# Transposes on TensorE from the third chunk on, filler matmuls in the first chunk, and one pool of four PSUM banks for the expert matmuls

## The chip, the cores and the metric

The kernel runs on one core of one Trainium2 chip. A core has five engines that this kernel uses: TensorE (PE) for matmuls, VectorE (DVE), ScalarE (ACT), GpSimd (POOL), and SyncE (SP), whose queue issues transfers. The metric is the device time of one execution in microseconds. Less is better. Three runs of the kernel before took 315.59, 315.67 and 315.96 us; the median is 315.67.

## The reference

Two stages follow each other. The first is a gated linear attention over 4 batches, 8 heads, 768 positions and a head size of 48. For each batch and head it keeps a 48 x 48 state:

```
f = sigmoid(f_logit)
for t in range(768):
    state = f[t][:, None] * state + outer(k[t], v[t])
    y[t]  = q[t] @ state
```

The 8 heads' outputs are put side by side, so that x has 4 x 768 = 3072 rows of 384. The second stage is a mixture of 4 experts, each with 1024 hidden units, in which every row goes through every expert:

```
p = domain_probs / (domain_probs.sum(-1) + 1e-9)
for e in range(4):
    out += p[:, e:e+1] * (relu(x @ w1[e]) @ w2[e])
```

Inputs and output are 32-bit floats in DRAM. The kernel casts operands of its matmuls to bf16 and accumulates in 32-bit.

## The kernel before

The 768 positions are cut into 6 chunks of 128. Within a chunk the attention is computed without a loop over positions: the logarithms of the gates are summed up by a matmul with a triangular matrix, queries are multiplied by the exponential of the sum and keys by its inverse, and two matmuls then give the chunk's output, with the state carried from chunk to chunk. Heads are handled in pairs, each padded to 64 columns, so a pair takes 112 partitions (MP).

One batch of one chunk goes through these steps (names of the plan, then the function):

- gate1, gate2 (ScalarE): log(1 + exp(-f)).
- cs (`pe_cs`, TensorE): cumulative sums, one matmul of 384 columns and, but for the last chunk, four of one column.
- exps (ScalarE): exponentials of both signs.
- q, k (`product`, L257, on GpSimd, or VectorE in chunks 0 and 1) and v (`cast_v`, L261): operands in bf16. The products of one batch share one padded tile `qk`; seven of these exist.
- The transpose of Q and K into the tile `QK`. In chunks 0 and 1 it is eight TensorE transposes (`pe_tp`, L265: tpq and tpk) into one PSUM bank and a copy by VectorE (ev_tp, L214). From chunk 2 on it is one DMA transpose from SP's queue (`dma_tp`, L269).
- at (`pe_at`, L280) and its masking by VectorE (ev_at, L284), y (`pe_y`, L291 and L295) and its cast to bf16 (ev_y).
- The transpose of the output into `xT`, the experts' operand. In chunks 0 and 1 it is three TensorE transposes (`pe_xt`, L320) and a copy (ev_xt, L212); from chunk 2 on one DMA transpose (`dma_xt`, L273).
- kv, ev_kv and state (`pe_kv`, L301, `ev_kv`, L308, `state`): the state for the next chunk.

The experts of one chunk work on all 512 rows (4 batches of 128). A unit h (`mm_h`, L324) is three matmuls of 512 columns into one PSUM bank, emptied by relu (`relu`, L332 on ScalarE, L330 on VectorE); in chunk 1 the first two experts are done in halves of 256 columns. A unit o (`mm_o`, L336) is four matmuls of 384 columns; two units with the same bank make one output tile, which `ev_o` (L343, L345, L347) scales and adds up. For one chunk that makes 32 h units (96 matmuls of 512 columns) and 32 o units (128 matmuls of 384 columns), which alternate over most of the span.

PSUM has eight banks, which the kernel hands out as rooms: two for h (`ps_h`), two for o (`ps_o`), four for the attention (`ps_t`).

The order is not written by hand. `Plan` is a small list scheduler that runs while the program is built. Each step has a cost in us for each engine that may do it, steps that it depends on, rooms that it takes and frees, a lag until its result can be used, and a priority. Going forward in planned time, `Plan.run` gives every idle engine the first step by priority whose inputs are there (0.2 us later for another engine, `LATENCY`) and whose rooms are free. The steps are then emitted in the order of planned start (L518 and after). The order on each engine's queue is thus the plan's; at run time an instruction waits for its inputs and everything behind it on that queue waits too.

The numbers of the plan that matter here: a load of one batch costs 1.05 us of DMA with a lag of 2.0, a gate step 0.54, cs 0.36, exps 1.1, the k product 0.56 on VectorE, tpq and tpk 0.22 each, at 0.35, y 0.28 in chunk 0 and 0.4 later, xt 0.17, kv 0.22, h 0.645, o 0.645, one expert weight 4.8 of DMA with a lag of 2.0.

`attention(c, ...)` adds a chunk's steps with priorities that spread them between the expert units of the chunk before; `zip_units` numbers those units. Chunk 0's attention has nothing to run beside. Its 16 loads of one batch each come first on SP's queue, the expert weights follow from GpSimd's queue after the last k load, and the loads of chunk 1 behind the sixth weight.

Of the kernel before, what the change touches and what calls it, by code (L numbers as in the profile page):

```python
# [14 lines left out]
class Op:  # L15


    def __init__(self, name, costs, emit, prio, deps=(), takes=(), frees=(), lag=0.0):
        self.name, self.costs, self.emit, self.prio = name, costs, emit, prio
        self.deps = [d for d in deps if d is not None]  # L20
        self.takes, self.frees, self.lag = list(takes), list(frees), lag
        self.end = self.start = self.engine = None


# [73 lines left out]
def kernel(  # L98
# [11 lines left out]
    nc = tc.nc  # L110
# [20 lines left out]
    ps = ctx.enter_context(tc.tile_pool(name="ps", bufs=1, space=PS))  # L131
    rooms = {"ps_h": 2, "ps_o": 2, "ps_t": 4, "f": 4, "q": 4, "k": 4, "v": 4, "ex": 2, "gp": 4, "e": 2, "qk": 7,
             "vb": 7, "egs": 8, "QK": 2, "AT": 2, "yb": 2, "xT": 2, "h": 2, "o": 8}
# [12 lines left out]
    pads = {}  # L146
    for nm, nb in (("gp", 2), ("qk", 2)):
        for i in range(rooms[nm]):
            t = pads[nm, i] = const.tile([T, nb, H, P2], BF16, name=f"{nm}{i}")
            nc.vector.memset(t[:, :, :, D:P2], 0.0)  # L150
# [22 lines left out]
    for nm, a in (("f", f_logit), ("q", q), ("k", k), ("v", v)):  # L173
# [5 lines left out]
        "ex": ([T, 2 * H, D], FP32), "e": ([T, 2, HD], FP32), "egs": ([MP, NP], FP32), "vb": ([T, H, D], BF16),  # L179
        "QK": ([128, 2, NP, T], BF16), "AT": ([T, 2, NP, T], BF16), "yb": ([T, HD], BF16),  # L180
        "xT": ([128, KD, NT], BF16), "h": ([128, KF, NT], BF16), "o": ([128, Din], FP32),
        "cs": ([T, 512], FP32), "tp": ([MP, 2, NP, T], BF16), "A": ([T, NP, T], FP32), "y": ([T, 512], FP32),
        "KV": ([T, 512], FP32), "xp": ([T, KD, T], BF16), "ps_h": ([128, NT], FP32), "ps_o": ([128, 512], FP32),
    }

    def tl(kind, *key):

        if (kind, key) not in tiles:
            room = kind if kind in rooms else "ps_t"
            slot = P.slot[(room, kind) + key if room == "ps_t" else (room,) + key]  # L190
            if room in ("gp", "qk"):
                tiles[kind, key] = pads[room, slot]
            else:
                shape, dt = shapes[kind]
                pool = ps if room.startswith("ps_") else wk
                tiles[kind, key] = pool.tile(shape, dt, name=f"{room}{slot}")
        return tiles[kind, key]
# [58 lines left out]
    def product(c, b, j, eng):  # L256
        engines[eng].tensor_tensor(out=tl("qk", c, b)[:, j, :, 0:D], in0=tl("qk"[j], c, b // 2)[:, hh(b), :],  # L257
                                   in1=tl("e", c, b)[:, j].rearrange("t (h d) -> t h d", d=D), op=ALU.mult)
# [4 lines left out]
    def pe_tp(c, b, j):  # L263
        for i in range(NP):
            nc.tensor.transpose(out=tl("tp", c, b)[:, j, i, :], in_=flat(tl("qk", c, b)[:, j], i)[:, 0:MP],  # L265
                                identity=ident)

    def dma_tp(c, b):
        nc.sync.dma_start_transpose(out=tl("QK", c, b).rearrange("m j i t -> m (j i) t"),  # L269
                                    in_=tl("qk", c, b).rearrange("t j h d -> t (j h d)"))  # L270

    def dma_xt(c, b):
        nc.sync.dma_start_transpose(out=tl("xT", c)[:, :, b * T:(b + 1) * T], in_=tl("yb", c, b))  # L273

# [12 lines left out]
    def pe_y(c, b):  # L287
        y, AT, vb, QK = tl("y", c, b), tl("AT", c, b), tl("vb", c, b), tl("QK", c, b)
        for i in range(NP):
            if c > 0:  # L290
                nc.tensor.matmul(out=y[:, i * 2 * D:(i + 1) * 2 * D], lhsT=QK[0:MP, 0, i, :],  # L291
                                 rhs=Sb[c % 2][:, b, i, :], start=True, stop=False, skip_group_check=True)
            for r in range(2):
                h = 2 * i + r
                nc.tensor.matmul(out=y[:, h * D:(h + 1) * D], lhsT=AT[:, r, i, :], rhs=vb[:, h, :],  # L295
                                 start=(c == 0), stop=True, skip_group_check=True)

    def pe_kv(c, b):
        kp, vb = tl("qk", c, b)[:, 1], tl("vb", c, b)
        for i in range(NP):  # L300
# [21 lines left out]
    def mm_h(c, e, fc, n0, n1):  # L322
        for kk in range(KD):
            nc.tensor.matmul(out=tl("ps_h", c, e, fc, n0)[:, n0:n1], lhsT=w1_sb[:, e, kk, fc * 128:(fc + 1) * 128],  # L324
                             rhs=tl("xT", c)[:, kk, n0:n1], start=(kk == 0), stop=(kk == KD - 1))

    def relu(c, e, fc, n0, n1, eng):
        dst, src = tl("h", c, e)[:, fc, n0:n1], tl("ps_h", c, e, fc, n0)[:, n0:n1]
        if eng == "DVE":
# [4 lines left out]
    def mm_o(c, e, nt, half):  # L334
        for fc in range(half * 4, half * 4 + 4):
            nc.tensor.matmul(out=tl("ps_o", c, e, nt)[:, 0:Din], lhsT=tl("h", c, e)[:, fc, nt * T:(nt + 1) * T],  # L336
                             rhs=w2_sb[:, e, fc, :], start=(fc == 0), stop=(fc == KF - 1))

    def ev_o(c, e, nt, eng):
        op, o = tl("ps_o", c, e, nt)[:, 0:Din], tl("o", c, nt)  # L340
        pe = pn[:, nt * C + c, e:e + 1]
# [39 lines left out]
    def attention(c, slot, gran):  # L381
# [10 lines left out]
        for b in range(B):  # L392
# [10 lines left out]
            qm = P.add(f"q {c}.{b}", pe, one(product, 0), s(4) - 0.2,  # L403
                       deps=[ex, ld[c, "q", b]], takes=[("qk", c, b)], frees=[("q", c, half), ("e", c, b)])
            km = P.add(f"k {c}.{b}", pe, one(product, 1), s(4) - 0.1,
                       deps=[ex, ld[c, "k", b]], takes=[("qk", c, b)], frees=[("k", c, half), ("e", c, b)])
            vb = P.add(f"v {c}.{b}", {"POOL": 0.5, "DVE": 0.36} if c < 2 else {"POOL": 0.5}, one(cast_v), s(4),
                       deps=[ld[c, "v", b]], takes=[("vb", c, b)], frees=[("v", c, half)])
            if c < 2:
                tq = P.add(f"tpq {c}.{b}", {"PE": 0.22}, on(pe_tp, 0), s(4), deps=[qm],  # L410
                           takes=[pt_("tp")], frees=[("qk", c, b)], lag=0.2)
                tk = P.add(f"tpk {c}.{b}", {"PE": 0.22}, on(pe_tp, 1), s(4) + 0.01, deps=[km],
                           takes=[pt_("tp")], frees=[("qk", c, b)], lag=0.2)
                et = P.add(f"ev_tp {c}.{b}", {"DVE": 0.69}, lambda e, b=b: copy(e, tl("QK", c, b)[0:MP], tl("tp", c, b)), s(4) + 0.1,
                           deps=[tq, tk], takes=[("QK", c, b)], frees=[pt_("tp")])
            else:
                et = P.add(f"tp {c}.{b}", {"DMA": 1.8}, on(dma_tp), s(4), deps=[qm, km], takes=[("QK", c, b)],
                           frees=[("qk", c, b)], lag=2.2)
            at = P.add(f"at {c}.{b}", {"PE": 0.35}, on(pe_at), s(7), deps=[et],
# [7 lines left out]
                       deps=[y], takes=[("yb", c, b)], frees=[pt_("y")])  # L427
            if c < 2:
                xt = P.add(f"xt {c}.{b}", {"PE": 0.17}, on(pe_xt), s(13), deps=[ey],
                           takes=[pt_("xp")], frees=[("yb", c, b)], lag=0.2)  # L430
                xdone[c, b] = P.add(f"ev_xt {c}.{b}", {"ACT": 0.48, "DVE": 0.4},
                                    lambda e, b=b: copy(e, tl("xT", c)[:, :, b * T:(b + 1) * T], tl("xp", c, b)),
                                    s(13) + 0.1, deps=[xt], takes=[("xT", c)], frees=[pt_("xp")])
            else:
                xdone[c, b] = P.add(f"xt {c}.{b}", {"DMA": 0.9}, on(dma_xt), s(13), deps=[ey], takes=[("xT", c)],
                                    frees=[("yb", c, b)], lag=2.2)
            if more:
                kv = P.add(f"kv {c}.{b}", {"PE": 0.22}, on(pe_kv), s(15), deps=[km, vb, y],
                           takes=[pt_("KV")], frees=[("vb", c, b), ("qk", c, b)], lag=0.2)
                ek = P.add(f"ev_kv {c}.{b}", {"DVE": 0.74}, on(ev_kv), s(15) + 0.1,  # L440
# [8 lines left out]
    def add_h(c, e, fc, n0, n1, xs):  # L449
        p, n = unit[0], n1 - n0  # L450
        key = ("ps_h", c, e, fc, n0)
        m = P.add(f"h {c}.{e}.{fc}.{n0}", {"PE": 0.645 * n / NT}, lambda _: mm_h(c, e, fc, n0, n1), p,
# [6 lines left out]
    def add_o(c, e, nt, half):  # L459
        p = unit[0] + 0.5  # L460
        key = ("ps_o", c, e, nt)
        d = [hdone[k] for k in hdone if k[:2] == (c, e) and half * 4 <= k[2] < half * 4 + 4 and k[3] <= nt * T]
# [47 lines left out]
    zip_units([], ol(C - 1, E - 1, ALL))  # L510

    done = P.run()
    if PRINT:
        PRINT(done)
    for o in done:
        o.emit(o.engine)

# [32 lines left out]
```

## Time and profile before

| what | value |
|---|---|
| median of three runs | 315.67 us |
| profiled execution | 315.96 us, its span 314.1 us |
| TensorE busy | 295.3 us, 94% of the span |
| ScalarE, VectorE, GpSimd busy | 163.0, 132.5, 92.6 us |
| first attention matmul | 4.89 us |
| first expert matmul | 25.38 us |
| DMA transposes | 16 into QK, 16 into xT |

PE is TensorE's matmuls, PEld its weight loads, which run beside matmuls. A matmul's duration in the profile includes the time in which its last results drain, in which the next one already runs; so the rate is read from starts, not durations. In a row of the timeline, the columns are the start, the duration from the first to the last instruction of a merged row, the engine, the line, the operation, output<-inputs, and the count; in square brackets stands the idle time before it and what ended it. In a table by stage each engine has its busy time and, in brackets, its number of instructions. The chain that ended last is a list of pieces: start, length, what.

### The profile page before, as it was taken

What the parts mean: (1) busy time and instruction counts of PE and PEld (TensorE: products, weight loads), DVE (VectorE), ACT (ScalarE), POOL (GpSimd) and SP (SyncE); (2) the same over time, 40 slices, a digit from 0 to 9 for tenths busy, and PEclk for the clock granted to TensorE, in tenths of its full rate; (3) what the DMA queues carried; (4) which work ended last, traced back from release to release, by engine and by line L of the source; (5) the groups of instructions that cost most, each with busy time, mean ns of one, the idle gap of its engine ahead of it and who ended that gap; (6) DMA issues with size and microseconds to landing.
All of it is one profiled execution on the core that took longest, in us unless ns stands there. A gap on an engine that the chain in (4) does not pass through costs nothing.

```text
span 314.1 us, 5415 instructions
## 1 busy us (share of the span) xinstructions
PE 295.3 (94%) x2098; PEld 171.1 (54%) x2128; DVE 132.5 (42%) x249; ACT 163.0 (52%) x310; POOL 92.6 (29%) x160
## 2 busy tenths in 40 slices
PE   1978999998999999999999999999999999999995
PEld 1753455556876555655555555555555555555552
DVE  6791002379954466443553222554332442201223
ACT  5634664554767563667544456443466444465430
POOL 4695000026996333860322200223322200000000
PEclk9999999999999999999999999999999999999999
DMA  8999999999999087999692113200322200200002
GB/s 156 211 150 192 196 208 201 208 202 214 189 223 236 6 172 140 230 197 189 108 196 48 50 50 48 46 15 13 95 75 46 50 13 15 75 25 2 0 0 100
DMA packets 135081, 36.05 MB, mean 115 GB/s; under 512 B 126352, under 2 KB 133520, under 8 KB 135056
## 3 DMA queue, kind: packets, MB, share of 16 engines
q1 hardware_dynamic: 129296, 29.42, 49.2%
q0 software_dynamic: 5760, 6.29, 12.0%
q8 instruction: 16, 0.26, 0.4%
q14 instruction: 9, 0.07, 0.1%
HBM read 31.51 MB, written 4.72 MB: 115 GB/s over the span
## 4 chain that ended last, share of the span: by engine, by line
PE 88%; DVE 7%; issue 2%; ACT 1%; DMA 1%; DVEq 0%; ACTq 0%
PE ps_h L324 40%; PE ps_o L336 39%; PE ps_t L280 2%; DVE qk L257 2%; DVE AT L284 2%; PE ps_t L295 1%; PE ps_t L244 1%; PE ps_t L291 1%; PE ps_t L301 1%; PE ps_t L247 1%; DMA f<-in_f_logit_dram 1%; PE ps_t L265 1%; DVE QK L214 1%; DVE o L343 1%; DVE vb L261 1%
## 5 line engine op out<-in xcount | busy, mean ns | idle before, releaser
L332 ACT ACTIVATE h<-ps_h 128x512 bf16<-128x512 f32 (+1 forms) x176 | 101.7, 579 | 111.2 <-PE ps_h L324 104.1
L324 PE MATMUL ps_h<-xT,w_sb 128*128 128x512 bf16 (+1 forms) x594 | 154.0, 367 | 2.9 <-ACT xT L212 0.6
L336 PE MATMUL ps_o<-w_sb,h 128*128 128x384 bf16 x768 | 153.0, 326 | 0.2
L336 PEld LDWEIGHTS <-h 128*128 128x128 bf16 x768 | 72.0, 98 | 56.8
L343 DVE SCALAR_TENSOR_TENSOR o<-ps_o,pn,o 128x384 f32<-128x384 f32 x72 | 44.4, 617 | 109.2 <-PE ps_o L336 101.9
L324 PEld LDWEIGHTS <-w_sb 128*128 128x128 bf16 x624 | 60.5, 99 | 50.9 <-issue 6.5
L284 DVE TENSOR_TENSOR AT<-ps_t,mask 128x512 bf16<-128x512 f32 x48 | 31.2, 684 | 14.8 <-PE ps_t L280 14.7
L261 POOL CAST vb<-v 128x384 bf16<-128x384 f32 x20 | 10.7, 537 | 72.9 <-DMA v<-in_v_dram 36.5
L257 POOL TENSOR_TENSOR qk<-q,e 128x384 bf16<-128x384 f32 x21 | 21.2, 1014 | 30.2 <-ACT e L251 29.9
L315 POOL TENSOR_TENSOR Sf<-Sf,egs 48x192 f32<-48x192 f32 x40 | 20.3, 508 | 24.6 <-DVE Sf L308 22.7
L330 DVE TENSOR_SCALAR h<-ps_h 128x256 bf16<-128x256 f32 (+1 forms) x32 | 17.4, 549 | 23.6 <-PE ps_h L324 23.2
L257 POOL TENSOR_TENSOR qk<-k,e 128x384 bf16<-128x384 f32 x19 | 19.3, 1015 | 21.8 <-ACT egs L254 11.3
L308 DVE TENSOR_TENSOR Sf<-Sf,ps_t 48x192 f32<-48x192 f32 x40 | 13.9, 349 | 10.7 <-PE ps_t L301 10.0
L251 ACT ACTIVATE e<-ps_t 128x384 f32<-128x384 f32 x24 | 11.8, 491 | 10.5 <-PE ps_t L247 4.6
L345 ACT ACTIVATE o<-ps_o,pn 128x384 f32<-128x384 f32 x22 | 12.8, 580 | 5.2 <-PE ps_o L336 4.5
L214 DVE CAST yb<-ps_t 128x384 bf16<-128x384 f32 x17 | 9.5, 556 | 13.8 <-PE ps_t L295 12.4
L316 POOL CAST sb<-Sf 48x192 bf16<-48x192 f32 x40 | 13.5, 339 | 2.6
L295 PE MATMUL ps_t<-vb,AT 128*128 128x48 bf16 x192 | 12.5, 190 | 1.5 <-DVE AT L284 1.4
L244 PE MATMUL ps_t<-gp,Ub 128*128 128x384 bf16 x24 | 8.5, 355 | 5.4 <-ACT gp L240 4.9
L295 PEld LDWEIGHTS <-AT 128*128 128x128 bf16 x192 | 10.5, 101 | 4.3 <-DVE AT L284 2.1
L252 ACT ACTIVATE e<-ps_t 128x384 f32<-128x384 f32 x24 | 11.9, 494 | 0.0
L236 ACT ACTIVATE ex<-f 128x768 f32<-128x768 f32 (+1 forms) x14 | 10.5, 753 | 1.9 <-DMA f<-in_f_logit_dram 1.7
(44 smaller groups left out, 138.7 us busy)
## 6 DMA issues: line engine op xcount, KB each, us to landing
w_sb<-in_moe_w_dram POOLq DMA_DIRECT2D x8, 768.0 KB, 20.9
out_dram<-o SPq DMA_DIRECT2D x24, 192.0 KB, 1.9
k<-in_k_dram SPq DMA_DIRECT2D x10, 384.0 KB, 5.3
f<-in_f_logit_dram SPq DMA_DIRECT2D x10, 384.0 KB, 5.6
q<-in_q_dram SPq DMA_DIRECT2D x10, 384.0 KB, 5.2
v<-in_v_dram SPq DMA_DIRECT2D x10, 384.0 KB, 5.8
f<-in_f_logit_dram SPq DMA_DIRECT2D x4, 192.0 KB, 3.9
k<-in_k_dram SPq DMA_DIRECT2D x4, 192.0 KB, 3.9
```

Source lines behind the costliest of these rows:

```text
L257: engines[eng].tensor_tensor(out=tl("qk", c, b)[:, j, :, 0:D], in0=tl("qk"[j], c, b // 2)[:, hh(b), :], in1=tl("e", c, b)[:, j].rearrange( ...
L261: engines[eng].tensor_copy(out=tl("vb", c, b), in_=tl("v", c, b // 2)[:, hh(b), :])
L284: nc.vector.tensor_tensor(out=tl("AT", c, b)[:, r].rearrange("s i t -> s (i t)"), in0=tl("A", c, b, r).rearrange("s i t -> s (i t)"), in1= ...
L295: nc.tensor.matmul(out=y[:, h * D:(h + 1) * D], lhsT=AT[:, r, i, :], rhs=vb[:, h, :], start=(c == 0), stop=True, skip_group_check=True)
L308: nc.vector.tensor_tensor(out=Sf[rows, b], in0=Sf[rows, b], in1=KV[rows, :, r, :], op=ALU.add)
L315: nc.gpsimd.tensor_tensor(out=Sf[rows, b], in0=Sf[rows, b], in1=eg, op=ALU.mult)
L316: nc.gpsimd.tensor_copy(out=nb[rows, b, :, r * D:(r + 1) * D], in_=Sf[rows, b])
L324: nc.tensor.matmul(out=tl("ps_h", c, e, fc, n0)[:, n0:n1], lhsT=w1_sb[:, e, kk, fc * 128:(fc + 1) * 128], rhs=tl("xT", c)[:, kk, n0:n1], s ...
L330: nc.vector.tensor_relu(out=dst, in_=src)
L332: nc.scalar.activation(out=dst, in_=src, func=AF.Relu)
L336: nc.tensor.matmul(out=tl("ps_o", c, e, nt)[:, 0:Din], lhsT=tl("h", c, e)[:, fc, nt * T:(nt + 1) * T], rhs=w2_sb[:, e, fc, :], start=(fc = ...
L343: nc.vector.scalar_tensor_tensor(out=o, in0=op, scalar=pe, in1=o, op0=ALU.mult, op1=ALU.add)
```

## The change

- Rooms: `ps_h` and `ps_o` become one room `ps_m` of four banks. An h unit takes one of these, an o unit too.
- The shared tile `qk` (7 of them) becomes two: `qp` (6) for queries and `kp` (7) for keys, each freed by its own last reader.
- `dma_tp` and `dma_xt` are gone. All chunks take the way that chunks 0 and 1 had: tpq, tpk, ev_tp, xt and ev_xt. `QK` has 112 partitions instead of 128.
- After planning, the new code walks through TensorE's steps in planned order up to the first h unit and puts filler matmuls before each of them: as many as the planned gap since the step before has multiples of 0.2 us, counted from 1.0 us. A filler is a 128 x 128 by 128 x 256 matmul of a constant tile `busy`, set to one by VectorE after the other constants, into the fourth of the `ps_m` banks. Nothing reads its result.

```diff
-    rooms = {"ps_h": 2, "ps_o": 2, "ps_t": 4, ..., "e": 2, "qk": 7,
+    rooms = {"ps_m": 4, "ps_t": 4, ..., "e": 2, "qp": 6, "kp": 7,
...
-    for nm, nb in (("gp", 2), ("qk", 2)):
+    for nm, nb in (("gp", 2), ("qp", 1), ("kp", 1)):
...
-    def dma_tp(c, b):
-        nc.sync.dma_start_transpose(out=tl("QK", c, b).rearrange("m j i t -> m (j i) t"),
-                                    in_=tl("qk", c, b).rearrange("t j h d -> t (j h d)"))
-
-    def dma_xt(c, b):
-        nc.sync.dma_start_transpose(out=tl("xT", c)[:, :, b * T:(b + 1) * T], in_=tl("yb", c, b))
...
-            if c < 2:
-                tq = P.add(f"tpq {c}.{b}", {"PE": 0.22}, on(pe_tp, 0), s(4), deps=[qm], ...)
-                tk = P.add(f"tpk {c}.{b}", {"PE": 0.22}, on(pe_tp, 1), s(4) + 0.01, deps=[km], ...)
-                et = P.add(f"ev_tp {c}.{b}", {"DVE": 0.69}, ...)
-            else:
-                et = P.add(f"tp {c}.{b}", {"DMA": 1.8}, on(dma_tp), s(4), deps=[qm, km], takes=[("QK", c, b)],
-                           frees=[("qk", c, b)], lag=2.2)
+            tq = P.add(f"tpq {c}.{b}", {"PE": 0.22}, on(pe_tp, 0), s(4), deps=[qm],
+                       takes=[pt_("tp")], frees=[("qp", c, b)], lag=0.2)
+            tk = P.add(f"tpk {c}.{b}", {"PE": 0.22}, on(pe_tp, 1), s(4) + 0.01, deps=[km],
+                       takes=[pt_("tp")], frees=[("kp", c, b)], lag=0.2)
+            et = P.add(f"ev_tp {c}.{b}", {"DVE": 0.69}, lambda e, b=b: copy(e, tl("QK", c, b), tl("tp", c, b)), s(4) + 0.1,
+                       deps=[tq, tk], takes=[("QK", c, b)], frees=[pt_("tp")])
...
-                xdone[c, b] = P.add(f"xt {c}.{b}", {"DMA": 0.9}, on(dma_xt), s(13), deps=[ey], takes=[("xT", c)],
-                                    frees=[("yb", c, b)], lag=2.2)
+            xt = P.add(f"xt {c}.{b}", {"PE": 0.17}, on(pe_xt), s(13), deps=[ey],
+                       takes=[pt_("xp")], frees=[("yb", c, b)], lag=0.2)
+            xdone[c, b] = P.add(f"ev_xt {c}.{b}", {"ACT": 0.48, "DVE": 0.4}, ...)
...
-        key = ("ps_h", c, e, fc, n0)
+        key = ("ps_m", "hp", c, e, fc, n0)
...
-        key = ("ps_o", c, e, nt)
+        key = ("ps_m", "op", c, e, nt)
...
     done = P.run()
+    first = next(o for o in done if o.name.startswith("h 0.")).start
+    busy = wk.tile([128, 256], BF16, name="busy")
+    nc.vector.memset(busy, 1.0)
+    spare = ps.tile([128, 512], FP32, name="ps_m3")
+    t = 1.0
+    for o in done:
+        if o.engine == "PE" and o.start <= first:
+            o.pad, t = int((o.start - t) / 0.2), o.end
     if PRINT:
         PRINT(done)
     for o in done:
+        for _ in range(o.pad):
+            nc.tensor.matmul(out=spare[:, 0:256], lhsT=busy[:, 0:128], rhs=busy, start=True, stop=True)
         o.emit(o.engine)
```

## The prediction

> **What bounds the kernel now.** I read the page's share of busy time and its 40 slices first, then busy time by stage, the order of instructions on TensorE, and the chain of waits in the first 26 us. Every time is us from the start of the one profiled execution: span 314.1, time 315.96, so 1.86 lies around the span; the median 315.67 is 0.29 (0.1%) lower.
>
> The page, with TensorE's and VectorE's slices of 7.85 us:
>
> ```profile
> PE 295.3 (94%) x2098; PEld 171.1 (54%) x2128; DVE 132.5 (42%) x249; ACT 163.0 (52%) x310; POOL 92.6 (29%) x160
> PE   1978999998999999999999999999999999999995
> DVE  6791002379954466443553222554332442201223
> PEclk9999999999999999999999999999999999999999
> ```
>
> TensorE is the resource; VectorE is full only in slices 2 and 3 and again in slices 8 to 10. Busy time by stage (engine by engine, then granted clock, DMA share, GB/s):
>
> ```profile
> 24.30:36.00 11.70, 10.79 (x37) 4.34 (x39) 0.62 (x3) 6.45 (x11) 4.07 (x10) 1.00 1.19 194
> 36.00:62.00 26.00, 25.84 (x140) 13.83 (x142) 3.72 (x7) 14.37 (x24) 0.50 (x1) 1.00 1.20 205
> 62.00:80.00 18.00, 16.06 (x178) 11.18 (x177) 15.83 (x28) 9.62 (x23) 8.80 (x13) 1.00 1.22 203
> 80.00:104.00 24.00, 23.33 (x217) 17.66 (x217) 13.79 (x32) 16.43 (x42) 17.98 (x27) 1.00 0.98 204
> 104.00:262.00 158.00, 156.90 (x1134) 87.00 (x1154) 69.69 (x123) 81.58 (x148) 44.40 (x78) 1.00 0.46 89
> ```
>
> The first number after each comma is TensorE. From 104 to 262, where nearly all of chunks 2 to 5's attention lies, it idles 1.10 us of 158. Work added to TensorE there lengthens the kernel by its own size; work taken from the DMA there is worth nothing. Before 24.3 TensorE waits for the first chunk's attention, a chain over all engines.
>
> **The transposes: about +9.6.** For each batch of chunks 2 to 5 (16 batches) the change removes two DMA transposes and adds on TensorE eight transposes of Q and K and three of x, with two evictions. Chunk 1 already does this, on a warm TensorE (start, duration, what):
>
> ```profile
> 74.16 0.61 PE L265 MATMUL ps_t<-ident,qk 128*112 128x128 bf16 x8
> 74.61 0.81 PE L336 MATMUL ps_o<-w_sb,h 128*128 128x384 bf16 x4
> ...
> 85.27 0.33 PE L320 MATMUL ps_t<-ident,yb 128*128 128x128 bf16 x3
> 85.44 0.49 PE L324 MATMUL ps_h<-xT,w_sb 128*128 128x256 bf16 x3
> ```
>
> A matmul's duration holds a drain that the next one overlaps, so I price by start to start: eight cost 74.61 - 74.16 = 0.45, three cost 0.17, a batch 0.62, sixteen 9.9. The same stretch's idle time could take up 1.1 at the very most; I let it take 0.3. Lower end 8.8, upper 9.9, I take 9.6.
>
> [...] The row gives 0.45/8 = 56 ns. [...]
>
> The evictions: the QK copy (0.68 on VectorE) and the xT copy (0.48 on ScalarE), 16 each, are 10.9 and 7.7 over 158 us in which the two are busy 69.7 and 81.6. They are hidden by the expert matmuls queued meanwhile. If one delayed an expert eviction so that both banks of its kind were full, TensorE would wait a fraction of a copy: 0 to 0.2 a batch, 0 to 3 in all. I take 0, since chunk 2's stage has idle engines and four shared banks tolerate more lateness. The DMA transposes leave SP's queue (issue 1.2 each, landing in 3.2 and 2.4), which frees loads and stores behind them; TensorE's waits in 104 to 262 name no transfer, so 0.
>
> **The head: fillers and a cold TensorE.** The clock row says full speed, but weight loads and spacing say otherwise:
>
> ```profile
> 30.02 0.15 PEld L324 LDWEIGHTS <-w_sb 128*128 128x128 bf16 x1 [0.28 <-issue]
> 30.45 0.15 PEld L324 LDWEIGHTS <-w_sb 128*128 128x128 bf16 x1 [0.28 <-issue]
> 30.88 1.01 PEld L324 LDWEIGHTS <-w_sb 128*128 128x128 bf16 x5 [0.28 <-issue]
> ```
>
> Until 30.88 a 512-column matmul takes 0.43 and its weight load 0.15; later 0.215 and 0.10. From the first expert matmul at 25.38 to the first output matmul at 35.84 lie 33, which take 10.46 against 33 x 0.215 = 7.10 warm: 3.4 lost, of which about 2.75 is cold running (13 at half rate), the rest a late second matmul and pauses between pairs of units (two h banks). A warm TensorE with four shared banks gains up to 3.4.
>
> [...] The rows show 5.5 us of cold experts, so I use the rows.
>
> Against this stands what fillers cost. A filler has 256 columns: half of 0.43 cold, 0.213; half of 0.215 warm, 0.108. The planner counts one per 0.2 of planned gap. For the first cs its costs give: load 1.05 + lag 2.0 + latency 0.2, gates 0.54 + 0.05 + 0.54, latency 0.2 = 4.58, minus 1.0 is 3.58, so 17 fillers. For the next transpose: exps from 5.34 to 6.44, k product from 6.64 to 7.20, plus 0.2 = 7.40 against cs's end 4.94: 12. Over the whole head, planned h cannot start before 24.1 (17.1 of loads, 4.8, 2.2), less 1.0 and 4 x 1.82 of TensorE work: 15.8 of gaps, about 70 fillers after rounding.
>
> The chain now, and where the first filler can start (the memset of its operand stands on VectorE behind the other memsets, which end at 4.89):
>
> ```profile
> 4.85 0.04 issue
> 4.89 0.48 PE ps_t L244
> 5.37 0.30 PE ps_t L247 x4
> ...
> 6.59 1.09 DVE qk L257
> 7.69 0.04 issue
> 7.73 0.67 PE ps_t L265 x4
> ```
>
> cs runs as soon as its gate is done. With fillers, 17 x 0.213 = 3.6 stand ahead of it from about 5.2: cs starts near 8.9, 4.0 late. The exponentials, the second batch's gates (behind them on ScalarE), the products and transposes all shift. The second block, 12 x 0.213 = 2.6 at most, ends near 12.2 against a chain ready at 11.7: 0 to 0.5 more. By then TensorE has run without pause for 6 us and should be warm.
>
> How much of the 4.0 survives to 25.38? VectorE limits it. From its first product (6.59) to its last mask product (end 23.18) pass 16.6, of which 2.3 idle. Started at 10.5 and packed tighter it ends between 25.3 and 27.1, 2.1 to 3.9 late. Warm transposes and y matmuls also shorten the last links by about 0.4. So the first expert matmul comes 1.5 to 4 late; lower end 1.1 early (the first weights, issued at 16.32 and landing in 8.0, hold it to 24.3). I take 2.2, nearer the VectorE bound. Later fillers run at 0.108 against planned gaps of 0.2 and hide in them. POOL's weight issue shifts with its products by about as much; the last of these weights lands by 56 now, chunk 1's loads follow behind the sixth (46.6), and POOL's v cast at 60.0 stands 5 before the k product that needs it, so 2 later hides.
>
> Head: +2.2 - 3.4 = -1.2, with ends -4.5 and +1.0.
>
> **Banks and rest.** In 62 to 104 TensorE idles 2.6. Mostly VectorE is full there, so sharing can return 0 to 0.6; I take 0.1. The split of qk's pads leaves the memsets about equal: 0.
>
> **Sum.** +9.6 - 1.2 - 0.1 = +8.3 on 315.96 gives 324.3; on the median 324.0.
>
> **Rivals.**
> (a) Fillers free: load waits and warm links swallow the late start, so the whole 3.4 is gained and the head gives about -3 to -4.5: 315.7 + 9.6 - 4 = 321.3. For: 2.3 of VectorE idle, links that halve. Against: 17 cold fillers in front of a matmul that today waits for nothing.
> (b) TensorE stays cold in the head, or fillers fill real gaps too: 70 x 0.213 = 15 beside about 14 of cold attention work (8.0 to 24 is busy 13.3) in a head of 20 leaves h some 9 late, less 0.7 for banks: 315.7 + 9.6 + 8 = 333. Against: 6 us of continuous work before 12.
> (c) Evictions stall TensorE in chunks 2 to 5, up to 0.2 a batch: 324 + 3 = 327. For: VectorE and ScalarE each pass 50% there; against: no eviction stalls it now.
> (d) Faster: transposes fall into gaps. The whole change is faster only if a batch's transposes cost TensorE less than 1.3/16 = 0.08 where the row gives 0.62, with the head at my value; with the head at its best (-4.5), below 0.28. Idle time of 1.1 over the stretch can't hold that. With a transpose cost of 0.05 a batch it would be 315.7 + 0.8 - 1.3 = 315.2.
> (e) The fillers don't warm the clock for the experts, or the plan drops them: head 0, 315.7 + 9.6 = 325.3; inside the main range.
>
> **Chances.** Main case with (e) 66%, (a) 14%, (b) 6%, (c) 11%, (d) 3%. The main case alone is 322 to 326.5. The range 320.8 to 328 reaches over (a) and (c) and leaves out (b), (d) and tails. About 0.2% is what a measurement here tells from no change. Faster takes (d)'s 2%, same 1%, slower 97%.
>
> **What would show it.** Right: 128 transposes of Q and K more on TensorE and 48 of x, 0.45 and 0.17 start to start; TensorE idle in chunks 2 to 5 still about 1%; 17 fillers before the first cs, which starts near 8.9; first expert matmul near 27.6 with weight loads of 0.10; stretch from first expert matmul to the end about 6 longer. Wrong: first expert matmul at or before 25.4 (a), weight loads of 0.15 past 12 us (b), new TensorE waits for the copies (c). My weakest number is how much of the late cs survives.

## The result

The changed kernel takes 325.25 us (median of four runs, 324.35 to 325.25) against 315.63 for the kernel before on the same chip: ratio 1.0298, 95% interval 1.0277 to 1.0320. The forecast was 324.0 in a range of 320.8 to 328.0. The total is inside the range, but two of its three terms were wrong by more than one microsecond each, in opposite directions. Ratios and their intervals leave out slow runs, those more than 1.5% above the fastest of their kernel; there are two, both of e7, and its median over all ten runs includes them.

The profiled execution took 325.25 us with a span of 323.5. First the page, with the shares and the slices (8.09 us each) of TensorE and VectorE, and the granted clock:

```profile
PE 308.7 (95%) x2352; PEld 185.0 (57%) x2383; DVE 142.0 (44%) x272; ACT 168.3 (52%) x326; POOL 93.1 (29%) x160
PE   3899999998999999999999999999999999999995
DVE  4593003379687334344654343555343543201223
PEclk9999999997999999999999999999999999999999
```

TensorE is busy 13.4 us longer than before. One slice has a clock of 0.7, which the kernel before never shows. Busy time by stage (same columns as above; the first two cuts are moved to the first expert matmul and the first o unit, the last lies 11 us later than before):

```profile
27.60:37.40 9.80, 9.73 (x46) 4.39 (x46) 0.00 (x0) 8.25 (x15) 3.41 (x9) 1.00 1.21 198
37.40:62.00 24.60, 24.48 (x134) 13.30 (x136) 4.11 (x7) 11.99 (x21) 0.00 (x0) 1.00 1.20 206
62.00:80.00 18.00, 16.15 (x169) 11.45 (x169) 14.51 (x26) 9.91 (x21) 8.26 (x11) 0.91 1.27 213
80.00:104.00 24.00, 24.00 (x315) 19.30 (x312) 18.33 (x41) 18.30 (x46) 20.03 (x37) 1.00 1.12 220
104.00:273.00 169.00, 167.79 (x1226) 96.68 (x1248) 75.32 (x133) 85.86 (x161) 43.88 (x72) 1.00 0.23 48
```

TensorE idles 1.2 of 169 us in the long stretch, as before, with the copies of the transposes now on VectorE and ScalarE. From 62 to 80 it is no better than before: 1.85 idle, and part of it at a clock of 0.91 instead of 1.00.

The head of the changed kernel, by TensorE's timeline (start, duration, what):

```profile
5.20 3.81 PE L512 MATMUL ps_m<-busy 128*128 128x256 bf16 x17 [5.20 <-DVE busy L502]
8.80 0.53 PE L245 MATMUL ps_t<-gp,Ub 128*128 128x384 bf16 x1
...
9.47 1.61 PE L512 MATMUL ps_m<-busy 128*128 128x256 bf16 x12
11.69 0.43 PE L266 MATMUL ps_t<-ident,kp 128*112 128x128 bf16 x4 [0.60 <-DVE kp L258]
...
26.94 0.71 PE L512 MATMUL ps_m<-busy 128*128 128x256 bf16 x5
27.67 9.87 PE L318 MATMUL ps_m<-xT,w_sb 128*128 128x512 bf16 x44
37.38 2.93 PE L330 MATMUL ps_m<-w_sb,h 128*128 128x384 bf16 x17
```

17 fillers hold the first cs until 8.80; 12 more lie ahead of the next transposes, which then wait 0.60 for VectorE all the same. 79 fillers run in all. The first expert matmul comes at 27.67 instead of 25.38, and the burst after it runs at full speed: 45 matmuls from 27.67 to 37.38 are 0.216 each (the trace lacks the record of one, so the row says 44).

The transposes in a chunk that had them on the DMA before:

```profile
93.59 0.33 PE L314 MATMUL ps_t<-ident,yb 128*128 128x128 bf16 x3
93.76 0.82 PE L318 MATMUL ps_m<-xT,w_sb 128*128 128x256 bf16 x6
94.41 0.39 PE L266 MATMUL ps_t<-ident,qp 128*112 128x128 bf16 x4
94.63 0.39 PE L266 MATMUL ps_t<-ident,kp 128*112 128x128 bf16 x4
94.86 0.49 PE L318 MATMUL ps_m<-xT,w_sb 128*128 128x256 bf16 x3
```

Eight cost 94.86 - 94.41 = 0.45 and three 0.17, to the digit what chunk 1's rows of the kernel before gave.

**One account for all kernels.** To see where time goes, I cut each trace at the first expert matmul, at the first expert weight load of chunk 1 (M), and at the last expert weight load. From the starts of TensorE's weight loads, which the traces hold for every expert matmul, "work" adds up what each matmul costs warm and back to back in these traces (0.216 for 512 columns, 0.163 for 384, 0.109 for 256, 0.056 for 128, half of that for the at matmuls, whose starts come in pairs, 3 to 4 ns apart in the changed kernel, 0.043 for 96, 0.025 for less). The durations that the rows give are longer by about 0.16 (medians in the changed kernel: 0.379 for 512 columns, 0.326 for 384). "Lost" is the elapsed time that is not work: waiting, half rate, and longer spacing where operations change (the eight at matmuls of 92.92 in the changed kernel take TensorE from 92.83 to 93.25, 0.42, against 8 x 0.028 = 0.22). A matmul that straddles a cut moves a sum by up to 0.2. The labels e1 to e5 are the experiments below.

```
                      first    lost     lost     M       from M to the last load
                      expert   26-36    62-80            elapsed  work    lost
before                25.38    3.04     4.05     79.54   230.16   224.17  5.99
changed               27.67    0.16     5.73     80.55   238.64   233.72  4.93
e1 no fillers         25.5     1.37     5.67     79.78   238.64   233.72  4.92
e2 fillers+banks      27.7     0.16     5.91     81.34   234.46   223.89  10.57
e3 banks only         25.4     2.23     5.84     80.67   230.07   223.89  6.18
e4 fillers only       27.3     1.89     4.05     79.92   231.66   224.17  7.49
e5 transposes only    25.6     2.33     4.17     78.95   238.87   233.99  4.88
```

The change's 9.5 us in the trace (last load at 319.20 against 309.70) are 1.0 before M and 8.5 after it.

### The profile page after: what moved, and what is told of

The parts are those of the page before. It is cut to its first block, busy times and chain, and to the rows that moved or that the text cites. A ratio compares the mean times of both kernels' runs of the same rounds, so it can differ in the third digit from the quotient of the medians.

```text
span 323.5 us, 5921 instructions
## 1 busy us (share of the span) xinstructions
PE 308.7 (95%) x2352; PEld 185.0 (57%) x2383; DVE 142.0 (44%) x272; ACT 168.3 (52%) x326; POOL 93.1 (29%) x160
## 4 chain that ended last, share of the span: by engine, by line
PE 89%; DVE 7%; issue 2%; ACT 0%; DVEq 0%; ACTq 0%
PE ps_m L330 38%; PE ps_m L318 38%; PE ps_t L266 3%; DVE AT L278 2%; PE ps_t L274 2%; PE ps_m L512 2%; PE ps_t L289 1%; PE ps_t L314 1%; PE ps_t L245 1%; PE ps_t L285 1%; PE ps_t L295 1%; PE ps_t L248 1%; DVE kp L258 1%; DVE o L337 1%; DVE QK L215 1%
## 5 line engine op out<-in xcount | busy, mean ns | idle before, releaser
L326 ACT ACTIVATE h<-ps_m 128x512 bf16<-128x512 f32 (+1 forms) x178 | 101.8, 575 | 110.3 <-PE ps_m L318 99.6
L330 PE MATMUL ps_m<-w_sb,h 128*128 128x384 bf16 x768 | 151.7, 326 | 0.3
L318 PE MATMUL ps_m<-xT,w_sb 128*128 128x512 bf16 (+1 forms) x593 | 150.3, 362 | 1.4
L337 DVE SCALAR_TENSOR_TENSOR o<-ps_m,pn,o 128x384 f32<-128x384 f32 x72 | 44.3, 617 | 111.6 <-PE ps_m L330 110.4
L258 POOL TENSOR_TENSOR qp<-q,e 128x384 bf16<-128x384 f32 x21 | 21.3, 1016 | 98.5 <-ACT e L252 95.0
L215 DVE COPY QK<-ps_t 112x1024 bf16<-112x1024 bf16 x24 | 16.5, 687 | 16.1 <-PE ps_t L266 16.1
L324 DVE TENSOR_SCALAR h<-ps_m 128x512 bf16<-128x512 f32 (+1 forms) x30 | 16.9, 574 | 15.0 <-PE ps_m L318 14.5
L258 POOL TENSOR_TENSOR kp<-k,e 128x384 bf16<-128x384 f32 x20 | 20.1, 1004 | 3.7 <-ACT egs L255 3.6
L512 PE MATMUL ps_m<-busy 128*128 128x256 bf16 x79 | 14.0, 307 | 5.2 <-DVE busy L502 5.2
L339 ACT ACTIVATE o<-ps_m,pn 128x384 f32<-128x384 f32 x23 | 13.3, 580 | 8.1 <-PE ps_m L330 7.7
```

The lines of the kernel that those rows point to most:

```text
L215: engines[eng].tensor_copy(out=out, in_=in_)
L258: engines[eng].tensor_tensor(out=tl(("qp", "kp")[j], c, b)[:, 0, :, 0:D], in0=tl("qk"[j], c, b // 2)[:, hh(b), :], in1=tl("e", c, b)[:, j] ...
L318: nc.tensor.matmul(out=tl("hp", c, e, fc, n0)[:, n0:n1], lhsT=w1_sb[:, e, kk, fc * 128:(fc + 1) * 128], rhs=tl("xT", c)[:, kk, n0:n1], sta ...
L324: nc.vector.tensor_relu(out=dst, in_=src)
L326: nc.scalar.activation(out=dst, in_=src, func=AF.Relu)
L330: nc.tensor.matmul(out=tl("op", c, e, nt)[:, 0:Din], lhsT=tl("h", c, e)[:, fc, nt * T:(nt + 1) * T], rhs=w2_sb[:, e, fc, :], start=(fc == ...
```

## The experiments

**e1 to e4: the parts alone and together.** e1 is the changed kernel without the fillers; e2 is the kernel before with fillers and shared banks, so that against the changed kernel only the transposes (and the split of `qk`) differ; e3 has the shared banks alone, e4 the fillers alone.

```diff
 e1
-    first = next(o for o in done if o.name.startswith("h 0.")).start
...
-        for _ in range(o.pad):
-            nc.tensor.matmul(out=spare[:, 0:256], lhsT=busy[:, 0:128], rhs=busy, start=True, stop=True)
 e3 (e2 has the fillers as well)
-    rooms = {"ps_h": 2, "ps_o": 2, "ps_t": 4, ...
+    rooms = {"ps_m": 4, "ps_t": 4, ...
 e4
+    spare = ps.tile([128, NT], FP32, name="ps_h1")
...
+        for _ in range(o.pad):
+            nc.tensor.matmul(out=spare[:, 0:256], lhsT=busy[:, 0:128], rhs=busy, start=True, stop=True)
```

> The changed kernel without its filler matmuls; transposes on TensorE and the four shared banks stay. Theory (parts add up: transposes +9.8, fillers +2.3 for the late start and -2.8 for the warm experts, banks -0.7): 324.5 to 325.5 us, first expert matmul back at about 25.4, cold weight loads (0.15) until about 31. Rival (fillers are a clear gain, the transposes cost more than 9.9): 327 or more. Rival (fillers are a clear loss through the late start): 322.5 or less.

> The kernel before with fillers and the four shared banks; the DMA transposes stay. Theory: 315.6 - 1.2 = 314.4 us (313.6 to 315.2), since only the transposes' 9.6 to 9.9 is missing against the changed kernel (325.25, or 324.35 without its cold stretch at 74.7 to 78.1). Rival (the transposes cost less on TensorE and something else, such as evictions or the cold stretch, makes up the rest): 316 or more.

> The kernel before with the four shared banks alone. Theory: pauses between pairs of h units in the first burst vanish (0.6) and little else: 314.7 to 315.3 us. Rival (sharing changes the plan's order and gains in chunk 1 as well): 314 or less. Rival (no effect): 315.6.

> The kernel before with fillers alone (into an h bank). Theory: +2.3 for the late start, -2.8 to -3.2 for warm experts: 314.7 to 315.3 us, first expert matmul at 27.6. Rival (fillers free): 312.5 to 313. Rival (late start dominates): 317.

Measured, with the kernel before at 315.52 on that chip: e1 324.40 (ratio 1.0283, 1.0262 to 1.0304), e2 319.88 (1.0146, 1.0103 to 1.0188), e3 316.40 (1.0027, 1.0006 to 1.0048), e4 317.85 (1.0070, 1.0055 to 1.0085). Only e1 came near its forecast. Fillers alone and banks alone each make the kernel slower, and with DMA transposes the two together cost 4.4. The theory of two small gains before M falls.

e2 shows what my list of rivals lacked. At the start of chunk 2's experts, TensorE's timeline of e2 reads:

```profile
133.15 0.32 PE L245 MATMUL ps_t<-gp,Ub 128*128 128x384 bf16 x1
133.31 0.32 PE L248 MATMUL ps_t<-ones,gp 128*112 128x1 bf16 x4
135.60 7.69 PE L325 MATMUL ps_m<-xT,w_sb 128*128 128x512 bf16 x26 [1.97 <-DMA xT<-yb]
```

TensorE has nothing left to run until the last DMA transpose of x lands. With four shared banks the plan moves chunk 2's attention back against chunk 1's experts: its last y starts at 129.1 in e2 and 126.5 in e3 against 123.5 in the kernel before, and two transfers and their landings stand between the batch's products and the experts. In e3 the same wait is 1.2. The kernel before has none, and neither has the changed kernel, where the transposes on TensorE bring that y forward to 102.5. So shared banks and DMA transposes together make TensorE wait. What that costs is less clear: e3 has the wait as well and yet loses only 0.2 more after M than the kernel before, while e2 loses 4.6 more, with half-rate windows from 75.4 to 85.6 and, right after the wait, from 136.8 to 140.2. In either case e2 holds a loss that the changed kernel does not have, and what the changed kernel costs over it (5.4) is not the price of the transposes.

**e5: the transposes alone.** All chunks transpose on TensorE; banks two and two, no fillers; the split of `qk` stays. Against the kernel before:

```diff
-            if c < 2:
-                tq = P.add(f"tpq {c}.{b}", ...)
...
-            else:
-                et = P.add(f"tp {c}.{b}", {"DMA": 1.8}, on(dma_tp), ...)
+            tq = P.add(f"tpq {c}.{b}", {"PE": 0.22}, on(pe_tp, 0), ...)
...
```

> The kernel before with the transposes of all chunks on TensorE and nothing else of the change (banks two and two, no fillers). Theory (TensorE is full from 104 to 262, so 16 x 0.62 = 9.9 comes on top): 315.5 + 9.6 to 9.9 = 325.1 to 325.4 us. Rival (the transposes are worth only what the changed kernel costs over fillers and banks with DMA transposes, 325.25 - 319.88 = 5.4): 321. If the theory holds, the 319.88 contains a loss that the DMA transposes cause only together with the banks.

Measured: 324.03 (323.09 to 324.37), ratio 1.0257 (1.0226 to 1.0287) against 315.57. The rival of 321 falls; the theory was about 1.2 too high. In the account e5 has 233.99 - 224.17 = 9.8 more work after M, as expected, but 1.1 less lost. The relief lies mostly between 100 and 140, in chunk 2's attention: 2.2 lost before, 0.3 in e5 as well as in the changed kernel. Elapsed after M is within 0.3 for e5, e1 and the changed kernel (238.87, 238.64, 238.64): past M, neither banks nor fillers matter once the transposes are on TensorE.

Of the changed kernel's +3.0%, then, the transposes alone are 2.6% and the other two parts some 0.4% together. In total times the intervals of e5, e1 and the changed kernel overlap; that the rest is a loss and not a gain rests on M in the traces (78.95, 79.78, 80.55) and on e3 and e4.

**e6 to e8: is the late start the fillers' price?** e6 puts the memset of `busy` ahead of VectorE's others, so that the fillers start at 1.25; e7 does this with fillers alone on the kernel before; e8 drops the 17 first fillers.

```diff
 e6, e7
+    busy = wk.tile([128, 256], BF16, name="busy")
+    nc.vector.memset(busy, 1.0)
     pads = {}
...
 e8
+    next(o for o in done if o.engine == "PE").pad = 0
```

> The changed kernel with the memset of the fillers' operand moved ahead of VectorE's other memsets, so that the same 79 fillers start at about 1.2 instead of 5.2. Theory (17 cold fillers, 3.6 us, then end at about 4.9, when the first cs becomes ready): first cs at 4.9 to 5.2, first expert matmul at 25.0 to 25.6 instead of 27.67, and 2.0 to 2.4 less than 325.25: 322.9 to 323.3 us, or 322.0 to 322.5 if no cold window falls into chunk 1's attention. Rival (chunk 1's attention is bound by something that the early start doesn't move): 324.5 or more.

> The kernel before (DMA transposes, banks two and two) with early fillers. Theory: the 317.85 of fillers alone less 2.0 to 2.4: 315.4 to 315.9 us with the cold window in chunk 1's attention, 314.5 to 315 without; below the kernel before only in the second case. Rival (warm experts are worth their whole 3.4 once the start isn't late): 312.5.

> The changed kernel without the 17 fillers ahead of the first cs; the other 62 stay. Theory: first cs back at 4.9, first expert matmul at 25 to 26. If the remaining fillers still warm TensorE before its experts: 322.5 to 323.3 us; if they don't: 324.4, as without any filler. Rival (the late start is not what the fillers cost): 325.

Measured: e6 325.75 (ratio 1.0310, 1.0271 to 1.0350), e7 316.92 (1.0016, 0.9988 to 1.0044), e8 324.35 (1.0275, 1.0237 to 1.0313). In e6 the first cs starts at 4.86, as forecast, and yet nothing is gained. Here is TensorE in e6, with the last fillers and the first expert matmuls:

```profile
24.82 0.71 PE L512 MATMUL ps_m<-busy 128*128 128x256 bf16 x5
26.74 9.89 PE L320 MATMUL ps_m<-xT,w_sb 128*128 128x512 bf16 x45 [1.22 <-DMA w_sb<-in_moe_w_dram]
```

and in e4 and e7, at the first o unit:

```profile
36.20 0.97 PE L337 MATMUL ps_o<-w_sb,h 128*128 128x384 bf16 x5 [0.66 <-DMA w_sb<-in_moe_w_dram]
```

```profile
36.36 3.72 PE L339 MATMUL ps_o<-w_sb,h 128*128 128x384 bf16 x12 [2.02 <-DMA w_sb<-in_moe_w_dram]
```

What is late next are the expert weights. With an earlier attention the first expert matmul waits for its first weight (26.74 in e6). With warm experts the first o unit waits for expert 0's second weight, the third to be loaded. This lands at 36.2 in e4 and at 36.3 in e7, although e7 starts its head early; in the kernel before it lands at 33.9, where a cold TensorE reached the first o unit at 35.84, and in the changed kernel at 36.8, before the first o unit at 37.38. Why it lands later with fillers is not shown. In e7 the wait of 2.0 is also followed by 3.4 us at half rate (36.3 to 39.7). In e8 the first cs is back at 4.73 and the experts run warm, but VectorE waits 1.62 for a load of v before 18.93, and the first expert matmul comes at 27.08.

The forecasts of e6, e7 and e8 all fall, and the time of e6 is in its rival's range. That the late start costs nothing does not follow: half-rate windows (the next experiment is about these) lie in these runs as well, in e6's trace from 73.2 to 83.4. At one mean clock, 0.994 to 0.995, e6 took 324.26 (one run) and e8 323.44 and 324.02 (two), the changed kernel 325.25 (three runs, in another measurement). An earlier start may thus be worth about 1 us that late weights and half-rate windows take back; no run shows it alone.

**e9: fillers in chunk 1's attention.** In all four runs of e4 and e6 and three of four of the changed kernel the granted clock is below 0.996. In e1, e5 and the kernel before it is not, but for one run (0.995). The traces' clock records show why: the clock goes to half for 3.41 us in the changed kernel (74.7 to 78.1), for as long in e4 (80.3 to 83.7), and for 10.2 us in e6 (73.2 to 83.4). e9 puts two fillers ahead of each at and y step of chunk 1.

```diff
     def pe_at(c, b):
         QK = tl("QK", c, b)
+        if c == 1:
+            filler(tl("A", c, b, 0)[:, 0:2, :].rearrange("s i t -> s (i t)"))
...
+        if c == 1:
+            filler(y[:, 0:256])
```

> The changed kernel with two more fillers ahead of the at and of the y matmuls of each batch of chunk 1 (16 fillers, 1.7 us warm, into the PSUM tile that the step then overwrites), where TensorE waits for VectorE. Theory (the half-rate windows follow stretches of light TensorE work in chunk 1's attention, about 72 to 81 us): no half-rate window there in any run, 324.0 to 324.8 us. Rival (the windows have nothing to do with the load on TensorE): as many of them as before, 325.5 to 326.9 with the fillers' own time.

Measured: 326.15 (ratio 1.0347, 1.0326 to 1.0367; the kernel before 315.25). The clock was 0.997 to 1.000 in its four runs and the trace has no half-rate window between 7.9 and 321.9, which fits the theory that the fillers prevent it. It did not pay: M is at 80.28 against 80.55, and the time is in the rival's range, not in the theory's. By the account, the half-rate window of the changed kernel costs little where it lies. VectorE, the third number, is busy nearly all of the time there, while the clock falls to 0.58:

```profile
70.00:74.00 4.00, 3.13 (x46) 2.40 (x44) 4.00 (x8) 1.77 (x6) 1.08 (x2) 1.00 1.34 214
74.00:78.00 4.00, 3.61 (x41) 2.90 (x41) 3.86 (x9) 1.76 (x5) 3.86 (x6) 0.58 1.05 189
```

Lost time from 70 to 80 is 5.20 in the changed kernel and in e3, which have the window, and 5.20 in e1, which has not. Against this stands one run: the changed kernel took 324.35 at a clock of 0.999 and 325.25 in each of the three runs at 0.995. So the window may cost up to 0.9, and then it is all that the changed kernel takes over e1 (324.40). It costs more where it reaches into the experts after 80: from 80 to 90 e2 loses 2.79 and e4 1.85 where e1 loses 0.80 and the kernel before 0.39.

**e10 and e11: weights in the order of use.** The kernel before with early fillers, and each expert's second weight loaded right behind its first; e11 has the fillers of e9 as well.

```diff
-    nw = [(0, 1), (1, 1), (0, 2), (2, 1), (1, 2), (3, 1), (2, 2), (3, 2)]
+    nw = [(0, 1), (0, 2), (1, 1), (1, 2), (2, 1), (2, 2), (3, 1), (3, 2)]
```

> The kernel before with early fillers and the weights loaded in the order of their use (each expert's second weight right behind its first). Theory (with early fillers alone TensorE waited 2.0 at 34 to 36.4 for expert 0's second weight and then ran 3.4 at half rate): no wait for weights after the first, first expert matmul at about 26, 313.0 to 314.5 us where chunk 1's attention stays warm. Rival (the head is bound by the bytes of the weights in any order): 315 to 317.

> The same with two fillers ahead of the at and y matmuls of each batch of chunk 1. Theory: like the kernel without these, with no half-rate window in chunk 1: 312.8 to 314.3 us and a narrower spread. Rival (16 fillers cost their 1.7 and prevent nothing): 315 or more.

Measured: e10 314.38 (ten runs, 313.60 to 317.86; ratio 0.9982, 0.9956 to 1.0009), e11 314.94 (0.9991, 0.9974 to 1.0008), the kernel before 315.25. In e10's trace TensorE's matmuls wait 0.26 at most for a weight, and M is at 77.13, 2.4 earlier than before. With this a warm head is worth something in that run. But e10's runs spread over 4.3 us, and e11's trace, of a run of 316.52, has the wait again in spite of the new order:

```profile
32.56 0.81 PE L347 MATMUL ps_o<-w_sb,h 128*128 128x384 bf16 x4 [1.99 <-DMA w_sb<-in_moe_w_dram]
```

e10's median is inside its forecast, e11's outside, and neither is shown to be faster than the kernel before. No kernel tried here beats it beyond the measurement.

## Why the prediction was right, and where it was wrong

**The transposes: mechanism right, size 1.1 too high.** TensorE was full, and its added work after M is 9.5 (changed) to 9.8 (e5), against my 9.9. Of this I let gaps take 0.3; 1.1 went into gaps. I had bounded the room by TensorE's idle time from 104 to 262, 1.10, and that was the wrong measure: idle time hardly changed (1.10 of 158, then 1.21 of 169). By the account the kernel before loses 4.2 there, most of it while TensorE counts as busy, and the relief lies in chunk 2's attention (from 104 to 140, 1.7 lost before, 0.2 to 0.3 in the changed kernel and e5). What exactly the transposes on TensorE spare there is not shown. The rows of chunk 2 keep to 0.45 / 8 = 56 ns a transpose. No eviction stalls TensorE: rival (c) falls, from 106 to 273 no wait of a TensorE matmul is on record.

**The head's start: right.** First cs at 8.80 (forecast 8.9), first expert matmul at 27.67 (27.6), clock warm at 9.8, VectorE as the limit. 79 fillers ran where about 70 were counted, and no cost of the nine more shows. Two readings were off without effect: from its first product to its last mask product VectorE idled 2.95 of 16.59 us in the kernel before (13.64 busy), not 2.3, and its second full stretch is slices 9 to 11, not 8 to 10. Its last mask product ends at 25.7, inside the 25.3 to 27.1 that I gave. Rivals (a) and (b) fall with it.

**The warm burst: its size nearly right, its value too high.** Lost time from 26 to 36 fell by 2.9 (3.04 to 0.16), where I booked 3.4. But part of this hangs on when full speed comes without fillers, and that differs from trace to trace: at 31.0 in the kernel before, 30.4 in e3, 28.8 in e5, 28.7 in e1. Against e1, which has the shared banks too, the fillers save 1.2 (1.37 to 0.16), and their late start costs 2.1. By M it comes to 2.3 - 2.9 + 1.7 = +1.1, measured +1.0, forecast -1.3. The 1.7 is the growth of lost time from 62 to 80 (4.05 to 5.73). It is not the fillers': e4, which has these without the banks, loses 4.05 there.

**The banks: the failing step.** I wrote that sharing "can return 0 to 0.6" in 62 to 104, since VectorE is full there. e1, e2, e3 and the changed kernel all lose 5.7 to 5.9 in 62 to 80, e5, e4 and the kernel before 4.05 to 4.17: sharing costs about 1.6 there, with or without the rest. Part of it comes back in the first burst; M moves by 1.1 from the kernel before to e3, 0.8 from e5 to e1 and 0.6 from e4 to the changed kernel. What goes with it in every one of these traces is the order of TensorE's instructions. In e5 (two and two), chunk 1's attention begins with a cs (L245) at 63.13, and o units stand between its steps up to 74.65, as in the kernel before:

```profile
63.13 0.33 PE L245 MATMUL ps_t<-gp,Ub 128*128 128x384 bf16 x1
...
64.46 2.11 PE L330 MATMUL ps_o<-w_sb,h 128*128 128x384 bf16 x12
...
71.65 0.81 PE L330 MATMUL ps_o<-w_sb,h 128*128 128x384 bf16 x4
72.39 0.40 PE L274 MATMUL ps_t<-QK 48*128 48x128 bf16 x8
72.72 0.82 PE L330 MATMUL ps_o<-w_sb,h 128*128 128x384 bf16 x4
...
74.00 0.81 PE L330 MATMUL ps_o<-w_sb,h 128*128 128x384 bf16 x4
```

In the changed kernel, with four banks, the plan runs them earlier: the twelve matmuls stand ahead of the cs, which starts 2.2 later (1.2 later than in e4, which has the fillers too), and no o unit is left between 70.7 and 80.6:

```profile
63.34 2.11 PE L330 MATMUL ps_m<-w_sb,h 128*128 128x384 bf16 x12
65.29 0.33 PE L245 MATMUL ps_t<-gp,Ub 128*128 128x384 bf16 x1
...
65.98 2.76 PE L330 MATMUL ps_m<-w_sb,h 128*128 128x384 bf16 x16
68.58 0.39 PE L266 MATMUL ps_t<-ident,qp 128*112 128x128 bf16 x4
...
70.09 0.81 PE L330 MATMUL ps_m<-w_sb,h 128*128 128x384 bf16 x4
...
80.58 0.49 PE L318 MATMUL ps_m<-xT,w_sb 128*128 128x256 bf16 x3
```

I looked at banks as slack at run time only; they also change what the scheduler sends first, so that the attention that VectorE paces begins later (its first cs at 64.7 to 65.5 in the four traces with shared banks, 63.1 to 64.1 in the three others) and the work that could have covered it is gone when it comes. Half-rate windows are not the cause: e1 has none there. The later traces fit, with about 5.1 to 6.6 lost from 62 to 80 with four banks (e6, e8, e9; e9 without a half-rate window) and 2.6 to 3.8 with two and two (e7, e10, e11). But no run changed the order alone, so that link is argued from the traces, not shown. (The loop that emits the steps is at L515, not at L518 as the description of the kernel has it.)

**What would have been nearer.** That the total came out 1.25 above the forecast is partly luck: the transposes were booked 1.1 too dear, the banks 1.8 and the burst 0.5 too cheap. Rival (e), 325.3, names the measured time, but not for its reason: the fillers do warm the experts; the gain is lost elsewhere. The late transfers that I had judged to be hidden (weights and chunk 1's loads) were hidden in the changed kernel; they bound only variants (a weight in e4, e5, e6, e7 and e11, the DMA transposes in e2 and e3). What the fillers took away from 26 to 36 is 2.9 of 314 us, 0.9%.

## What to carry to other kernels

Before booking a gain in an early stage, ask which resource sets the next stage's pace: warm matmuls at 28 to 37 us brought no shorter kernel, since their fillers came at a price, the next weight could be late (36.2 in e4), and VectorE paces chunk 1's attention (busy 7.86 of the 8 us from 70 to 78 in the changed kernel). A freer buffer pool in a list scheduler is a change of order, and independent work may be worth most when it is kept for the stage that cannot fill TensorE. Where one engine is full, added work costs its start-to-start time, less the lost time that it displaces: here 8.7 of 9.8 (e5).

## What the hardware showed that I had not expected

Half rate also came where TensorE was mostly busy. In the changed kernel's clock record it lasts from 74.65 to 78.06; in the 3.41 us before, TensorE counts as busy for 2.15, with no wait longer than 0.71. The changes on record there lie whole multiples of 3.413 us from each other: half rate lasts 3.413, the full rate behind it 245.760, 72 times as long; in the kernel before full rate lasts 283.306, 83 times as long. So I cut each trace into stretches of that length, counted from a recorded change, and for stretches at full rate I added the columns of the matmuls that start in them, as a share of what full speed passes (512 columns in 0.2155 us). Of fourteen stretches with few columns nine were followed by half rate:

```
kernel    3.41 us from  share   the next 3.41 us
changed   71.2          0.33    half rate
e3        71.4          0.35    half rate
e4        76.9          0.40    half rate
e6        69.8          0.43    half rate
e7        32.8          0.32    half rate
e8        19.4          0.43    half rate
e8        70.6          0.33    half rate
e2        71.9          0.44    half rate
e2        133.4         0.32    half rate
e3        129.4         0.37    full rate
e1        76.5          0.43    full rate
before    75.3          0.47    full rate
e11       17.0          0.47    full rate
e10       72.3          0.51    full rate
```

The shares of the two kinds overlap: e3's from 129.4 is followed by full rate. Traces can lack records of matmuls; counted by weight loads, of which the experts' are all there, this one and e2's from 133.4 both have 0.44, and only e2's is followed by half rate. The count is good to a few hundredths, since a matmul that straddles a border is counted by its start. So the share alone does not tell here what follows, and what does is not shown. Half rate begins at different times from trace to trace (73.2 in e6, 74.7 in the changed kernel, 75.4 in e2, 80.3 in e4), and times mostly go with the mean clock, which each half-rate window lowers: of e3's ten runs two took 315.5 us at a mean clock of 0.997 and 0.998, six 316.1 to 317.2 at 0.992 to 0.993 and one 319.0 at 0.983; one of 316.5 at 1.000 falls out of this order. Why the kernel before has none, with a light stretch of its own at 75 to 79, while e4 with the same instructions there is below 0.995 in all four runs, stays open.

The clock row of the page reads full speed from the start, also before TensorE's first recorded change (31.0 in the kernel before), while weight loads of 0.15 and 512 columns in 0.43 show half.
